# Moving loads, casts and DMA transposes in a one-core attention and feed-forward kernel, with the last sum cut into three

## The chip, the core and the metric

The kernel runs on one core of a Trainium2 chip. The core has a matrix engine (TensorE, PE in the profile), three engines for elementwise work (VectorE or DVE, ScalarE or ACT, GpSimd or POOL), a queue engine that only issues transfers (SyncE or SP) and 16 DMA engines. SP, ACT and POOL can each issue transfers, in the order of their own instruction streams. Products are summed in PSUM; everything else lies in SBUF.

The metric is the device time of one execution in microseconds (us). Before the change the median of three runs is 236.67 us (236.6 to 236.97). The profiled execution took 236.38 us.

## The reference

```python
scores = np.matmul(q, k.transpose(0, 1, 3, 2)) / np.sqrt(64)
# head h keeps all earlier positions where is_retrieval[h] is 1, else only the
# first 4 positions and the last 64
scores = np.where(mask, scores, -1e9)
a = softmax(scores)                       # over the keys
x = np.matmul(a, v)                       # 4 batches, 8 heads, 768 positions, 64 wide
x = x.transpose(0, 2, 1, 3).reshape(3072, 512)
h = x @ w_in                              # 512 -> 2048
g = h / (1 + np.exp(-beta * h))
out = g @ w_out                           # 2048 -> 512
```

All inputs and the output are float32. Heads 0, 2 and 6 are retrieval heads, the other five stream. The kernel works in bfloat16 with float32 sums.

## The kernel before

**Units and chunks.** A chunk is half a sequence of one batch (384 rows, three tiles of 128); there are 8. A unit is one chunk of one pair of heads, so chunk c holds units 4c to 4c+3, and there are 32. A unit goes through these steps, each with its instructions written out in the order in which they are to run:

- its keys and queries are cast to bfloat16 (`cast`, line 273), transposed on TensorE (`steps_T`, line 354), and copied from PSUM: keys by DVE (line 355), the two heads' queries by ACT and DVE (line 360). This holds for units 0 to 11;
- `sinks_of` (lines 337, 338) copies, on POOL, the key tiles of streaming heads with the four first positions put in;
- `steps_QK`: score products (line 419), for units 0 to 7 a second product that adds the mask (line 425), the exponential on ACT (line 428), and from unit 8 masks multiplied on DVE (lines 435, 440). A unit's products are cut into fills of up to four blocks;
- `values`: v is cast (`cast_v`, line 279) and, on POOL, the streaming heads' copy is made (lines 289, 290);
- `steps_PV`: products with v (line 463), 6 steps, one for each head and tile; after the last DVE takes reciprocals and divides, which writes x (line 468);
- x is transposed, on TensorE (`steps_X`, line 495) for units 0 to 7, 11, 30 and 31, and by a DMA transpose on SP (`x_by_dma`, line 479) for the others.

When the four units of a chunk have x transposed, its feed-forward part can run: `steps_G1` (16 groups of four products, line 518, in the order of the pairs of heads; tanh on ACT, line 521; the gate on DVE, line 524) and `steps_G2` (line 561 or 544, then ACT copies to one of three output buffers `osb`, and a transfer goes out).

**The ramp** is units 0 to 7, written out by hand (lines 690 to 807). Keys and queries of a chunk come in two groups of four heads (`load_qk`), v in three transfers on SP (`load_v`). With `held=True` a small POOL memset into the target keeps a transfer from starting before POOL gets there. w_in and w_out are cast in transfers that POOL issues (`load_w_in`, `load_w_out`, four quarters each). Ten products on zeros (line 167) run before the first data.

**The slots** follow: `for t in range(8, NU + 2)` (line 810). Slot t holds the score products of unit t, the products with v of unit t-1, and some feed-forward steps, in a merged order. From chunk 3 on the rows of keys and queries are loaded by POOL with a cast (`load_rows`, 3 transfers of keys and 6 of queries a chunk) and transposed by SP (`transposes_dma`, lines 323 and 326, three each).

**What sets the order.** Each engine runs its instructions in the order in which the program emits them. A call in the text of a slot's top is emitted there. `later(delay, fn)` puts work off until the program's own clock, which adds up a planned cost for each TensorE step, has moved by `delay`. `x_by_dma` is put off by 700 from the last step of the products with v, so it is emitted early in the next slot. A planner (`next_m`) picks feed-forward steps. It takes a chunk's first group only some time after its last x was emitted.

Of the kernel before, what the change touches and what calls it, by code (L numbers as in the profile page):

```python
# [17 lines left out]
def kernel(  # L18
# [86 lines left out]
    def load_qk(c, g, pairs=1, held=False):  # L105

        b, h2 = chunks[c]
        rows = slice(h2 * HALF, (h2 + 1) * HALF)
        both = stage.tile([128, 2, 2, 2, HT, D], F32, name=f"s{g}")
        for i, (name, src) in enumerate((("k", k), ("q", q))):  # L110
            staged[name, c, g] = both[:, i]
            if held:
                nc.gpsimd.memset(staged[name, c, g][:, 0, 0, 0, 0:1], 0.0)
        n = 2 // pairs
        for i in range(pairs):
            for name, src in (("k", k), ("q", q)):
                h = 4 * g + 2 * n * i
                eng = nc.scalar if pairs == 2 and name == "q" else nc.sync
                eng.dma_start(
                    out=staged[name, c, g][:, n * i:n * (i + 1)].rearrange("p a h t d -> p (a h) (t d)"),  # L120
                    in_=src[b, h:h + 2 * n, rows, :].rearrange("h (p t) d -> p h (t d)", t=HT))
# [26 lines left out]
    load_qk(0, 1)  # L148
# [19 lines left out]
    idle(10, ps_m, "mm")  # L168
# [26 lines left out]
    def negatives():  # L195
        nc.vector.tensor_scalar(out=Mc, in0=Nc, scalar1=0.0, scalar2=None, op0=ALU.is_ge)
        for i, m in enumerate([M0, Mo, Md, Mo, Md]):
            nc.vector.tensor_scalar(out=Ns[:, i * 128:(i + 1) * 128], in0=m, scalar1=-1.0, scalar2=-NEG, op0=ALU.add, op1=ALU.mult)
# [38 lines left out]
    def zero_q(i):  # L237
        for hh in range(2):
            nc.vector.memset(QTB[i][hh][half(1 - hh), :], 0.0)
# [6 lines left out]
    for i in range(3):  # L246
        zero_q(i)
    ones_v(nc.vector, 0)
    ones_v(nc.gpsimd, 1)
# [25 lines left out]
    def cast_v(u):  # L275
        b, h2, p = units[u]
        c = u // NPAIR
        copy = nc.scalar.copy if u in (1, 3) else nc.vector.tensor_copy if 8 <= u < 16 else nc.gpsimd.tensor_copy
        copy(out=VX[b % 2, p][:, h2 * HT:(h2 + 1) * HT, :, 0:D], in_=staged["v", c][:, :, 2 * p:2 * p + 2, :])  # L279
# [66 lines left out]
    def steps_T(u):  # L346
# [3 lines left out]
        def go():  # L350
# [7 lines left out]
            for hh in range(2):  # L358
                copy = nc.vector.tensor_copy if hh and u != 4 else nc.scalar.copy
                copy(out=QT[hh][half(hh), :].rearrange("p (j t) -> p j t", t=HT),  # L360
                     in_=tq[half(hh)].rearrange("p t j -> p j t"))
# [168 lines left out]
    def steps_G2(c):  # L530
# [3 lines left out]
        def part(ns, f0, cols=None):  # L534
            def go():
                for f in gates[c]:
                    f()
                if cols is not None:
# [7 lines left out]
                    if f0 + 4 == FO:  # L546
                        n0 = (2 * chunks[c][0] + chunks[c][1]) * HALF + ns * 128
                        m = (z - a) // 2 if z == d_model else z - a
                        osb = moe.tile([128, d_model], F32, name="osb", bufs=3)
                        nc.scalar.activation(out=osb[:, 0:m], in_=op[:, 0:m], func=ACTF.Copy, scale=0.5)  # L550
                        nc.scalar.dma_start(out=out[n0:n0 + 128, a:a + m], in_=osb[:, 0:m])
                        if m < z - a:
                            osb = moe.tile([128, d_model], F32, name="osb", bufs=3)
                            nc.vector.tensor_scalar(out=osb[:, 0:m], in0=op[:, m:z - a], scalar1=0.5, scalar2=None, op0=ALU.mult)
                            nc.sync.dma_start(out=out[n0:n0 + 128, a + m:z], in_=osb[:, 0:m])
# [13 lines left out]
        for ns in range(HT):  # L569
            if c == NCHUNK - 1 and ns == HT - 1:  # L570
                for cols in ((0, 256), (256, 512)):
                    res += [part(ns, f0, cols) for f0 in range(0, FO, 4)]
# [117 lines left out]
    cast_dp(0)  # L690
    load_v(0, held=True)
    load_qk(1, 0)
    negatives()
    transposes_of(0)
    st_u[0]["sinks"]()
    cast(1, "k", act)
    cast(1, "q")
# [7 lines left out]
    cast_dp(3)  # L705
    qk = steps_QK(1)
# [10 lines left out]
    load_qk(1, 1, held=True)  # L717
    st_u[3]["sinks"]()
    run(steps_QK(3))
    load_v(1, held=True)  # L720
    step((100, beta_go))
    values(0)
    load_w_in(0)
    cast_dp(4)
    values(1)
    values(2)
    cast(5, "q")
    values(3)


    run(steps_PV(0))
    transposes_of(4)
    cast(5, "k", act)
    run(steps_PV(1))
    step(steps_X(0)[0])
    qk = steps_QK(4)
    step(qk[0])
    run(steps_PV(2))
    step(qk[1])
    step(steps_X(1)[0])  # L740
    cast(6, "k", dve)
    transposes_of(5)
    step(qk[2])
# [66 lines left out]
    for t in range(8, NU + 2):  # L810
# [91 lines left out]
```

## Time and profile before

| What | Value |
|---|---|
| time, median of 3 runs | 236.67 us (236.6 to 236.97) |
| time of the profiled execution | 236.38 us |
| its span, first to last instruction | 234.7 us |
| TensorE busy | 224.9 us (96%) |
| ScalarE, VectorE, GpSimd busy | 158.9, 149.0, 102.9 us |
| granted TensorE clock, mean | 0.999 |
| DMA: read, written | 27.27 MB, 6.29 MB |
| first product on zeros, first transpose, first score product | 1.29, 5.53, 6.63 us |
| first products of unit 4 with v | 25.53 us |
| last product ends | 231.2 us |

The span is what the profiler sees between the first and the last instruction; the time has 1.7 us more around it. Times in the traces count from the start of the span. A line of the timeline gives start, duration, engine, line of the code, operation, output and inputs; several instructions of a kind in a row are merged, with their number behind an x. "Idle before" names what the engine waited for. The list of DMA issues gives the time from issue to landing.

### The profile page before, as it was taken

The numbers are of one execution on the slowest core, as the hardware profiler recorded it, in microseconds if no ns is written. First come the engines' busy times: TensorE is split into PE (matmuls) and PEld (weight loads), VectorE is DVE, ScalarE is ACT, GpSimd is POOL, SyncE is SP. The second block draws the span as 40 slices with busy tenths as digits, with TensorE's granted clock in tenths as the row PEclk, the third lists the DMA queues.
The fourth block names the chain that finished last, engine by engine and source line by source line (L and its number), as shares of the span: only waits on it lengthen the run. The fifth ranks groups of instructions, "written<-read, shape, count | busy, mean of one in ns | idle before, by whom it ended". The sixth has DMA issues, their size and how long they took to land.

```text
span 234.7 us, 5275 instructions
## 1 busy us (share of the span) xinstructions
PE 224.9 (96%) x1920; PEld 138.8 (59%) x1920; DVE 149.0 (64%) x384; ACT 158.9 (68%) x309; POOL 102.9 (44%) x246
## 2 busy tenths in 40 slices
PE   7797899999999999999999999999999999999994
PEld 3676766655666675656555666566665666555553
DVE  6778779877768598647862776476671857345400
ACT  2897888847767799558772779577875876266521
POOL 6487760357749932597078607841470000000000
PEclk9999999999999999999999999999999999999999
DMA  6999999999999999899989996999321200201112
GB/s 201 260 295 195 183 169 229 228 214 233 155 197 130 203 194 151 124 170 149 230 118 158 172 218 85 135 180 158 90 64 61 63 18 2 77 13 46 46 47 89
DMA packets 103530, 33.75 MB, mean 144 GB/s; under 512 B 89920, under 2 KB 100560, under 8 KB 103504
## 3 DMA queue, kind: packets, MB, share of 16 engines
q1 hardware_dynamic: 66976, 24.68, 51.2%
q0 software_dynamic: 35664, 8.13, 40.9%
q10 hardware_dynamic: 864, 0.60, 0.8%
q8 instruction: 15, 0.25, 0.5%
q14 instruction: 11, 0.09, 0.1%
HBM read 27.27 MB, written 6.29 MB: 143 GB/s over the span
## 4 chain that ended last, share of the span: by engine, by line
PE 81%; DMA 7%; DVE 6%; ACT 3%; POOL 1%; issue 1%; ACTq 0%; POOLq 0%
PE mm L518 28%; PE tp L561 25%; PE mm L561 9%; PE sp L419 9%; PE po L463 4%; DMA w_in_sb<-in_moe_w_in_dram 4%; DMA QTD<-s 3%; DVE gT L524 2%; PE mm L167 2%; PE sp L518 2%; PE tp L354 1%; ACT th L521 1%; DVE x L468 1%; ACT esL L428 1%; PE tp L544 1%
## 5 line engine op out<-in xcount | busy, mean ns | idle before, releaser
L518 PE MATMUL mm<-xT,w_in_sb 128*128 128x384 bf16 x488 | 93.4, 326 | 1.0 <-DVE gT L524 0.5
L521 ACT ACTIVATE th<-mm,beta_h 128x384 f32<-128x384 f32 x122 | 71.1, 583 | 24.1 <-PE mm L518 19.4
L524 DVE SCALAR_TENSOR_TENSOR gT<-th,mm 128x384 bf16<-128x384 f32 x122 | 66.7, 552 | 27.2 <-ACT th L521 23.8
L561 PE MATMUL tp<-w_out_sb,gT 128*128 128x512 bf16 x272 | 67.2, 379 | 0.0
L518 PEld LDWEIGHTS <-w_in_sb 128*128 128x128 bf16 x512 | 46.5, 98 | 27.0 <-issue 0.7
L561 PEld LDWEIGHTS <-gT 128*128 128x128 bf16 x368 | 33.3, 98 | 28.1
L428 ACT ACTIVATE esL<-sp 128x384 bf16<-128x384 f32 x72 | 37.8, 542 | 15.4 <-PE sp L419 15.3
L419 PE MATMUL sp<-QTD,KT 128*128 128x128 bf16 (+2 forms) x261 | 45.6, 242 | 1.7 <-ACT es L428 0.8
L428 ACT ACTIVATE es<-sp 128x512 bf16<-128x512 f32 (+1 forms) x56 | 30.4, 560 | 6.7 <-PE sp L419 5.4
L419 PEld LDWEIGHTS <-KT 128*128 128x128 bf16 x272 | 24.8, 98 | 9.3 <-DVE KT L355 0.7
L561 PE MATMUL mm<-w_out_sb,gT 128*128 128x512 bf16 x96 | 24.1, 379 | 0.0
L279 POOL CAST VX<-vs 128x384 bf16<-128x384 f32 x22 | 11.3, 512 | 28.5 <-issue 14.5
L312 POOL DMA_DIRECT2D s<-in_q_dram x30 | 22.3, 749 | 1.4 <-issue 0.9
L337 POOL COPY KO<-KT 128x128 bf16<-128x128 bf16 (+1 forms) x32 | 12.9, 405 | 14.5 <-DVE KT L355 9.3
L463 PEld LDWEIGHTS <-esL 128*128 128x128 bf16 x252 | 14.5, 98 | 7.2
L463 PEld LDWEIGHTS <-es 128*128 128x128 bf16 x220 | 13.9, 98 | 7.4 <-issue 0.2
L565 ACT ACTIVATE osb<-tp 128x512 f32<-128x512 f32 x17 | 10.2, 597 | 11.8 <-PE tp L561 11.5
L435 DVE TENSOR_TENSOR es<-es,Mh 128x512 bf16<-128x512 bf16 (+2 forms) x30 | 11.6, 388 | 8.5 <-ACT es L428 8.4
L440 DVE TENSOR_TENSOR esL<-esL,Mc 128x128 bf16<-128x128 bf16 x36 | 9.1, 252 | 12.0 <-ACT esL L428 12.0
L468 DVE TENSOR_TENSOR x<-po,rec 128x384 bf16<-128x384 f32 x28 | 15.6, 557 | 1.0
L463 PE MATMUL po<-VX,esL 128*128 128x65 bf16 x216 | 16.0, 193 | 0.0
L419 PE MATMUL sp<-QTD,KO 128*128 128x128 bf16 x79 | 14.7, 219 | 0.0
(94 smaller groups left out, 232.7 us busy)
## 6 DMA issues: line engine op xcount, KB each, us to landing
vs<-in_v_dram SPq DMA_DIRECT2D x24, 256.0 KB, 5.2
out_dram<-osb SPq DMA_DIRECT2D x23, 256.0 KB, 2.9
w_in_sb<-in_moe_w_in_dram POOLq DMA_DIRECT2D x4, 512.0 KB, 8.1
w_out_sb<-in_moe_w_out_dram POOLq DMA_DIRECT2D x4, 512.0 KB, 11.5
s<-in_k_dram SPq DMA_DIRECT2D x5, 384.0 KB, 5.0
s<-in_q_dram SPq DMA_DIRECT2D x5, 384.0 KB, 5.8
s<-in_k_dram POOLq DMA_DIRECT2D x15, 128.0 KB, 5.8
s<-in_q_dram POOLq DMA_DIRECT2D x30, 64.0 KB, 4.6
```

What stands on the lines that cost most here:

```text
L279: copy(out=VX[b % 2, p][:, h2 * HT:(h2 + 1) * HT, :, 0:D], in_=staged["v", c][:, :, 2 * p:2 * p + 2, :])
L312: nc.gpsimd.dma_start(out=ROWS[c % 2, "q"][:, t, :, 3 * D * hh:3 * D * hh + D], in_=q[b, hh:H:2, r:r + 128, :].rearrange("h p d -> p h d"))
L337: nc.gpsimd.tensor_copy(out=ko[:, ka - 1:kz - 1, :], in_=kt[:, ka * 128:kz * 128].rearrange("p (a j) -> p a j", a=n))
L419: nc.tensor.matmul(sp[:, (i - lo) * 128:(j - lo) * 128], lst[i][1], s["QT"][lst[i][0]][:, q0 * 128:(q0 + j - i) * 128], start=True, stop=n ...
L428: nc.scalar.activation(out=es[:, lo * 128:hi * 128], in_=sp[:, 0:w], func=ACTF.Exp, scale=scale)
L435: nc.vector.tensor_mul(es[:, a * 128:z * 128], es[:, a * 128:z * 128], Mh[h2][:, m0 * 128:(m0 + z - a) * 128])
L463: nc.tensor.matmul(po[:, qi, hh, :], e, val, start=(j == 0), stop=(j == len(lst) - 1))
L468: nc.vector.tensor_mul(x, po[:, :, :, 0:D], rec.to_broadcast([128, HT, 2, D]))
L518: nc.tensor.matmul(hp[:, 0:HALF], w_in_sb[:, mo, fi * 128:(fi + 1) * 128], xT[c][:, mo, :], start=(mo == 0), stop=(mo == MO - 1))
L521: nc.scalar.activation(out=th, in_=hp[:, 0:HALF], func=ACTF.Tanh, scale=beta_h[:, fi:fi + 1])
L524: nc.vector.scalar_tensor_tensor(out=gTs[c][:, fi, :], in0=th, scalar=1.0, in1=hp[:, 0:HALF], op0=ALU.add, op1=ALU.mult)
L561: nc.tensor.matmul(op, gTs[c][:, fi, ns * 128:(ns + 1) * 128], w_out_sb[:, fi, :], start=(fi == 0), stop=(fi == FO - 1))
```

## The change

**Loads.** Units 2 and 3, and units 4 and 5, get their keys and queries in two pairs of transfers, one for each unit, all on SP. The first quarter of w_in is issued behind unit 2's sinks. v's and units 6's and 7's transfers of chunk 1 are released at other places of POOL's stream.

**Casts.** Unit 0's queries go from POOL to ACT, unit 1's keys from ACT to DVE, unit 1's v from ACT to DVE, unit 4's queries from POOL to DVE, unit 6's keys from DVE to POOL. ACT copies both halves of unit 0's transposed queries. The negative masks are made in two parts, unit 2's query buffer is zeroed by POOL, and the columns of ones are written later.

**The order of the ramp.** Unit 4's transposes stand inside unit 0's products with v, unit 5's inside unit 2's, so the last of these, and the division behind it, come later. Unit 6's come ahead of unit 3's x. There are 8 products on zeros instead of 10.

**Slots.** The rows of chunk 4 are loaded in slots 10 and 11 (before: 11 to 13), those of chunks 5 to 7 one slot sooner. Chunk 3's key and query transposes both stand at the top of slot 9 (before: 9 and 10), chunk 4's at 12 and 13 (before: 13 and 14). For chunks 5 to 7 the keys stand at the top of slots 17, 21 and 25, the queries at 18, 22 and 26; before, both stood at the latter.

**The last sum.** The last 128 rows of the output are summed in column ranges of 256, 128 and 128, each in a PSUM bank of its own; ACT, DVE and ACT copy them. Before, there were two ranges of 256, and ACT and DVE each copied half of the second.

```diff
@@ load_qk and the first loads
-                eng = nc.scalar if pairs == 2 and name == "q" else nc.sync
+                eng = nc.scalar if (c, g) == (0, 0) and name == "q" else nc.sync
...
-    load_qk(0, 1)
+    load_qk(0, 1, 2)
...
-    idle(10, ps_m, "mm")
+    idle(8, ps_m, "mm")
@@ cast_v and steps_T
-        copy = nc.scalar.copy if u in (1, 3) else nc.vector.tensor_copy if 8 <= u < 16 else nc.gpsimd.tensor_copy
+        copy = nc.scalar.copy if u == 3 else nc.vector.tensor_copy if u == 1 or 8 <= u < 16 else nc.gpsimd.tensor_copy
...
-                copy = nc.vector.tensor_copy if hh and u != 4 else nc.scalar.copy
+                copy = nc.vector.tensor_copy if hh and u not in (0, 4) else nc.scalar.copy
@@ steps_G2, last 128 rows
-                        m = (z - a) // 2 if z == d_model else z - a
-                        osb = moe.tile([128, d_model], F32, name="osb", bufs=3)
-                        nc.scalar.activation(out=osb[:, 0:m], in_=op[:, 0:m], func=ACTF.Copy, scale=0.5)
-                        nc.scalar.dma_start(out=out[n0:n0 + 128, a:a + m], in_=osb[:, 0:m])
-                        if m < z - a:
-                            osb = moe.tile([128, d_model], F32, name="osb", bufs=3)
-                            nc.vector.tensor_scalar(out=osb[:, 0:m], in0=op[:, m:z - a], scalar1=0.5, scalar2=None, op0=ALU.mult)
-                            nc.sync.dma_start(out=out[n0:n0 + 128, a + m:z], in_=osb[:, 0:m])
+                        osb = moe.tile([128, d_model], F32, name="osb", bufs=3)[:, 0:z - a]
+                        if a == 256:
+                            nc.vector.tensor_scalar(out=osb, in0=op, scalar1=0.5, scalar2=None, op0=ALU.mult)
+                        else:
+                            nc.scalar.activation(out=osb, in_=op, func=ACTF.Copy, scale=0.5)
+                        (nc.scalar if z == d_model else nc.sync).dma_start(out=out[n0:n0 + 128, a:z], in_=osb)
...
-                for cols in ((0, 256), (256, 512)):
+                for cols in ((0, 256), (256, 384), (384, 512)):
@@ the ramp
-    cast_dp(0)
+    negatives((0, 1, 3))
+    cast(0, "k", dve)
+    cast(0, "q", act)
     load_v(0, held=True)
-    load_qk(1, 0)
-    negatives()
+    load_qk(1, 0, 2)
+    zero_q(2, nc.gpsimd)
+    negatives((2, 4))
     transposes_of(0)
+    cast(1, "k", dve)
+    cast(1, "q")
     st_u[0]["sinks"]()
-    cast(1, "k", act)
-    cast(1, "q")
...
     cast_dp(2)
     cast_dp(3)
+    load_qk(1, 1, held=True)
+    ones_v(nc.vector, 0)
+    ones_v(nc.gpsimd, 1)
...
     st_u[2]["sinks"]()
-    load_qk(1, 1, held=True)
+    load_w_in(0)
+    load_v(1, held=True)
     st_u[3]["sinks"]()
     run(steps_QK(3))
-    load_v(1, held=True)
+    cast(5, "k", act)
+    values(0)
+    values(1)
+    cast(4, "k", dve)
+    cast(4, "q", dve)
     step((100, beta_go))
-    values(0)
-    load_w_in(0)
-    cast_dp(4)
-    values(1)
     values(2)
-    cast(5, "q")
-    values(3)
-
-
-    run(steps_PV(0))
+
+
+    pv = steps_PV(0)
+    run(pv[:5])
     transposes_of(4)
-    cast(5, "k", act)
+    run(pv[5:])
     run(steps_PV(1))
-    step(steps_X(0)[0])
     qk = steps_QK(4)
     step(qk[0])
-    run(steps_PV(2))
+    cast(5, "q")
+    cast(6, "k")
+    values(3)
+    cast(6, "q")
+    pv = steps_PV(2)
+    run(pv[:5])
+    step(steps_X(0)[0])
     step(qk[1])
+    transposes_of(5)
+    run(pv[5:])
+    step(qk[2])
     step(steps_X(1)[0])
-    cast(6, "k", dve)
-    transposes_of(5)
-    step(qk[2])
     run(steps_PV(3))
     step(steps_X(2)[0])
     qk = steps_QK(5)
     step(qk[0])
     step(qk[1])
+    cast(7, "q")
+    load_w_in(1)
+    transposes_of(6)
     step(steps_X(3)[0])
     step(qk[2])
-    load_w_in(1)
-    cast(6, "q")
-    cast(7, "q")
     load_w_in(2)
     load_w_in(3)
-    transposes_of(6)
     cast(7, "k", dve)
@@ the slots
-            c, i = (t + 5) // NPAIR, (t + 5) % NPAIR
-            some = load_rows(c)[3 * i:3 * i + 3] if c < NCHUNK else []
-            if t < 14:
-                some = load_rows(4)[{9: 0, 10: 0, 11: 0, 12: 4, 13: 8}[t]:{9: 0, 10: 0, 11: 4, 12: 8, 13: 9}[t]]
+            c, i = (t + 6) // NPAIR, (t + 6) % NPAIR
+            some = load_rows(c)[3 * i:3 * i + 3] if t >= 14 and c < NCHUNK else []
+            if t in (10, 11):
+                some = load_rows(4)[0:4] if t == 10 else load_rows(4)[4:9]
         for i, f in enumerate(some):
-            later(1000 + (1500 if t > 14 else 1000) * i, f)
+            later((2500 if t == 10 else 1000) + (1500 if t > 14 else 1000) * i, f)
...
         if t == 9:
-            transposes_dma(3, "k")
-        if t == 10:
-            transposes_dma(3, "q")
+            transposes_dma(3)
+        if t == 12:
+            transposes_dma(4, "k")
         if t == 13:
-            transposes_dma(4, "k")
-        if t == 14:
             transposes_dma(4, "q")
+        if t > 14 and t % NPAIR == 1 and t // NPAIR + 1 < NCHUNK:
+            transposes_dma(t // NPAIR + 1, "k")
         if t > 14 and t % NPAIR == 2 and t // NPAIR + 1 < NCHUNK:
-            transposes_dma(t // NPAIR + 1)
+            transposes_dma(t // NPAIR + 1, "q")
```

The cut parts give `negatives` a list of the masks to make and `zero_q` the engine, and take the earlier calls of `zero_q` and `ones_v` out.

More of the change, by code (lines that the diff above doesn't have):

```diff
@@ L193, with negatives @@
     nc.gpsimd.affine_select(out=Nc, in_=Nc, compare_op=ALU.is_ge, fill=NEG, base=0, pattern=[[1, 128]], channel_multiplier=-1)
-    def negatives():
-        nc.vector.tensor_scalar(out=Mc, in0=Nc, scalar1=0.0, scalar2=None, op0=ALU.is_ge)
-        for i, m in enumerate([M0, Mo, Md, Mo, Md]):
+    def negatives(which):
+        if 2 in which:
+            nc.vector.tensor_scalar(out=Mc, in0=Nc, scalar1=0.0, scalar2=None, op0=ALU.is_ge)
+        for i in which:
+            m = [M0, Mo, Md, Mo, Md][i]
             nc.vector.tensor_scalar(out=Ns[:, i * 128:(i + 1) * 128], in0=m, scalar1=-1.0, scalar2=-NEG, op0=ALU.add, op1=ALU.mult)
@@ L235, in half, with zero_q @@
         return slice(hh * D, (hh + 1) * D)
-    def zero_q(i):
+    def zero_q(i, eng):
         for hh in range(2):
-            nc.vector.memset(QTB[i][hh][half(1 - hh), :], 0.0)
+            eng.memset(QTB[i][hh][half(1 - hh), :], 0.0)
     def ones_v(eng, b):
@@ L244, in ones_v @@
             eng.memset(VO[b, p][:, :, :, D:D + 1], 1.0)
[L246 to L249, printed above, removed]
+    zero_q(0, nc.vector)
+    zero_q(1, nc.vector)
     def masks_late(h2):
```

## The prediction

> **What bounds the kernel now.** I read the page's busy shares first, then a table of stretches, then TensorE's waits, then the SP queue's own order.
>
> ```profile
> span 234.7 us, 5275 instructions
> PE 224.9 (96%) x1920; PEld 138.8 (59%) x1920; DVE 149.0 (64%) x384; ACT 158.9 (68%) x309; POOL 102.9 (44%) x246
> ```
>
> TensorE (PE) is the bound. The stretches show where its other 4% lies (columns: length, then busy time of PE, its weight loads, DVE, ACT, POOL, granted clock, DMA share, GB/s):
>
> ```profile
> 2.00:34.00 32.00, 27.84 (x341) 20.06 (x340) 24.26 (x69) 24.71 (x52) 23.85 (x78) 1.00 1.14 232
> 34.00:90.00 56.00, 56.00 (x482) 34.83 (x481) 43.55 (x109) 42.69 (x84) 31.48 (x59) 1.00 1.36 196
> 90.00:120.00 30.00, 29.18 (x240) 17.72 (x239) 20.54 (x60) 21.00 (x42) 14.38 (x33) 1.00 1.38 159
> 120.00:228.00 108.00, 108.00 (x835) 63.28 (x834) 59.47 (x145) 69.32 (x132) 32.32 (x71) 1.00 0.59 93
> ```
>
> So 4.2 us are idle in the ramp (2 to 34), 0.8 between 90 and 120, nothing elsewhere until the tail. A faster engine elsewhere buys nothing; a new wait costs its full length. The 0.8 is these two waits:
>
> ```profile
> PE mm L518 <- DVE gT L524: 0.5, 1, 0.5
> PE sp L419 <- DMA QTD<-s: 0.3, 1, 0.3
> ```
>
> The second is unit 20's first product at 116.05: the product before it was issued at 115.54 and takes 0.03 of the stream, so the stream stands for 0.5 us.
>
> The change moves DMA transposes on SP, so I looked at what else SP carries. The transposes of x (line 479) feed the first matrix product of the feed-forward part (line 518). Two of them, each with SP's issue before or behind it:
>
> ```profile
> 72.87 1.18 SPq L479 DMA_TRANSPOSE xT<-x  x1
> 76.23 4.51 SPq L323 DMA_TRANSPOSE KT<-s  x3
> ...
> 121.18 0.36 SPq L567 DMA_DIRECT2D out_dram<-osb  x1
> 123.20 1.18 SPq L479 DMA_TRANSPOSE xT<-x  x1
> ```
>
> And PE's products that read them:
>
> ```profile
> 80.23 0.81 PE L518 MATMUL mm<-xT,w_in_sb 128*128 128x384 bf16 x4
> ...
> 128.25 0.81 PE L518 MATMUL mm<-xT,w_in_sb 128*128 128x384 bf16 x4
> ```
>
> The first is unit 10's: issued at 72.87, when x has just been written, it lands 5.6 later (the list of DMA issues, cut to that moment), at 78.5. Line 518 multiplies the four pairs in order, 0.16 us each, and needs pair 2 at 80.55: 2.1 us to spare. The second is unit 19's (landing 4.2, at 127.4); it is needed as fourth, at 128.74: 1.3 to spare.
>
> Last, the two DMA queues when both have work (18 to 20 us, kind, packets, MB, share of the 16 engines; q0 is POOL's, q1 is SP's):
>
> ```profile
> q0 software_dynamic: 381, 0.39, 116.8%
> q1 hardware_dynamic: 90, 0.02, 6.7%
> ```
>
> While w_in's first quarter flows, SP's transfers nearly stand, though v's last rows are still queued (they land after 23). The share over 2 to 34 is 1.14: the DMA engines are full in the ramp, and whatever is put first pushes something back.
>
> **The change, part by part.** One profiled execution, 236.38 us (span 234.7 and 1.7 around it), is the base; it lies 0.3 below the median of the three runs, 236.67.
>
> *Ramp, to unit 4.* With 8 idle products instead of 10, PE is free 2 x 0.425 = 0.85 earlier, at 4.7. Unit 0's queries are cast on ACT (idle from 3.4 to 6.1) when they land at 4.5: 0.5, as POOL took. Keys go at 4.7, queries at 5.05, ACT copies both halves of the transposed queries (2 x 0.4), and the first product starts at 6.0 instead of 6.63. Unit 1's keys, cast on DVE after the key copy (5.75 to 6.3) and its queries on POOL ahead of the sinks (landed 5.6), let its transposes go at 6.35, not at 7.05 and 7.60. Unit 2's land alone, so its casts follow at 7.85 (DVE) and 7.75 (POOL): transposes at 8.4, not 9.69. From there ACT sets the pace, as now: its last exponential ends at 13.4, not 14.65. Then v must land (12.4 at the latest row), and DVE casts v of unit 1 and unit 4's keys and queries, 3 x 0.5: unit 4's transposes go at 13.95, against 14.85. Up to here 0.9 to 1.25 us are won. The masks' parts, the zeroing on POOL (about 0.35 each, from 1.43 for 1536 columns) and the ones lie beside these casts; without that cover the ones on DVE cost unit 2's key copy 0.35.
>
> *Ramp, w_in.* Its first quarter is now issued behind unit 2's sinks on POOL, at about 10.25 instead of 13.76. It flows 2.2 to 3.7 us after its issue (rows at 19.68 and 13.76), so from 12.4 to 13.9, and takes about 2.7 us of the engines. On SP, units 4 and 5 are just through by 13; units 6 and 7, now 15.35 (keys) and 16.6 (queries), land up to 2.7 later, the queries at 19.2. POOL's queue stands behind them: unit 6's casts are ahead of unit 3's values and, behind these, of unit 5's sinks, unit 7's queries and the other three quarters of w_in. From 19.2: cast 0.5, unit 6 transposed at 19.75 (now 21.26); sinks and cast 1.0, three issues 2.25, unit 6's sinks done at 23.45 (now 23.3). So POOL's chain ends as it does now, while PE reaches unit 6's second block at 23.45 instead of 23.87, and unit 4's products with v at 24.6 instead of 25.53. I take 0.9 us for the whole ramp. Best: unit 6's queries land at 16.6, as now; PE's own work up to unit 6 then lets the chain start about 1.3 sooner: -2.2. Worst: they, or v, land 1.4 later: +0.5. Behind 34 us the transfers start at the old times, but the earliest that PE meets (unit 9's cast at 53.75 for 55.01) leaves 1.2, so the 0.9 is kept.
>
> *Dividing unit 2 later* moves DVE's 0.7 behind unit 5's key copy; its x is read after 18 us either way: 0.
>
> *Rows on POOL.* Nine issues of 0.75 to 0.88 move from the slots of units 11 to 13 to those of 10 and 11, later chunks one slot on. POOL idles 1.9 us at 65 and 6.4 at 89.5: 0 to +0.2, taken 0. Chunk 3's query transposes now follow its keys, from 62.7 to 66.8, ahead of an output at 63.74; there are three output buffers and the next two are filled at 69 and 74: 0.
>
> *Key transposes a slot sooner.* They are issued at the top of a slot, and the transpose of the last finished unit's x comes 700 units of the program's clock into it: on SP the x now stands behind three key transposes. Four places:
> - Chunk 4's before unit 10's x. SP is free at 72.5, three take 4.0 to 4.5 (58.72 and 76.23), x is issued at about 76.75. It lands 4.0 (median) to 6.0 later (unit 12's, behind three others at 88.71): 80.75 to 82.75, needed at 80.55. I take 4.8 and so +1.0; bounds 0 (a landing of 3.8, as at 68.4) and +2.4.
> - Chunk 6's before unit 19's x. SP is free at 121.54; 3.99; x at 125.55, and 4.1 as unit 20's took behind six: 129.65 against 128.74, +0.9; bounds 0 (2.4, as at 161.7) and +1.2.
> - Chunk 5's and 7's before units 15 and 23: SP is idle from 95.1 and from 145.54, so x is only 0.9 late, and 1.5 and 2.0 are to spare: 0, at most +0.3.
>
> *Query transposes* start 4 us sooner for chunk 5: unit 20's wait goes, -0.5; next there is the gate product, on time.
>
> *Tail.* Three banks: 32 products of 128 columns take 32 x 0.0556 = 1.78 where 16 of 256 take 16 x 0.109 = 1.74: +0.05. The last piece now waits on ACT for the output buffer that DVE waits for now, until 231.56; then 0.28, an issue, and 1.6 to landing as before: 0 (-0.3 if the lone last transfer lands faster, +0.2 if the buffer is later).
>
> Sum: -0.9 + 1.0 + 0.9 - 0.5 + 0.05 = +0.55: 236.9 for the base, 237.2 for the median.
>
> [...] The idle products start 0.425 apart, later ones of 512 columns 0.217 (the granted clock reads 1.00 in both): half rate, for 4.2 us from the first product at 1.29 to about 5.5. [...]
>
> **Rivals.** 0.2% (0.47 us) is about what a measurement of this kernel tells from none.
> - *The x land in time* (faster). SP's key transposes are done sooner, or x behind them lands in 3.8 and 3.2: both terms go, 0.55 - 1.9 = -1.35: 235.3. It decides at landings of 80.55 and 128.74. For it: landings of 2.3 to 4.0 us where DMA is quiet. Against: 4 to 6 behind other transposes.
> - *w_in does not hold SP back* (faster). Unit 6's queries land before 17.5, the ramp gives -2.2: 235.9. Against: the two queue lines above.
> - *The ramp gives nothing*: 238.1. Unit 6's queries come 1 us later still, and POOL's chain with them, or v does. For it: full DMA engines.
> - *Half rate to 9* (slower): if the stream of 8 does not do, and 4.2 us count anew from its end at 4.7, PE runs at half until 8.9. Its 2.4 us of work from 5.5 on then take twice as long; the waits that lie there now (0.56 + 0.21 + 0.69) cover more than half. Unit 4 falls back to 14.85, and since unit 6's queries set the rest, the ramp keeps 0.5: 237.6. Against: transposes and products follow the stream at once.
> - *The x come half as late*: the terms cancel, 236.7.
>
> **How the numbers follow.** My forecast 0.42 (0.06 of it within 0.2%; its own range 236.8 to 238.0), x in time 0.27, w_in harmless 0.12 (0.02 within), no ramp gain 0.08, half rate 0.04, cancelled 0.07. Faster 0.37, within 0.15, slower 0.48. The likeliest gives 237.2; 8 in 10 reach from 235.0 to 238.4.
>
> **What would show it.** Right: SP issues chunk 4's keys near 72.5 and unit 10's x near 76.8; PE waits on a DMA of xT near 80 and 128, about 1 us each; no wait on QTD near 115; unit 2's first transpose near 8.4; w_in's first quarter issued near 10, unit 6's queries landing near 19. Wrong: no wait on xT, or a first wait on w_in or on POOL's casts after 13 us that is longer than 1 us.

## The result and the profile after

The changed kernel takes 238.0 us (median; 236.5 to 240.0) against 236.2 us for the kernel before in the same comparison: a ratio of 1.0070 with a 95% interval of 1.0048 to 1.0092, slower by 0.7%. The forecast was 237.2, "slower" at 0.48. The profiled execution took 238.08 us (span 236.4), 1.70 more than that of before, where the forecast's sum was +0.55. In 5 of its 18 executions the granted clock has a mean of 0.986 or 0.993 instead of 0.999 or 1.000; their median is 239.8, that of the others 237.6. An experiment below shows what stood ahead of three falls of the clock (1.45, 0.55 and 0.52 us of PE's work in a stretch of 3.41); in these five executions the cause was not traced.

The page:

```profile
span 236.4 us, 5286 instructions
PE 223.3 (94%) x1911; PEld 138.4 (59%) x1934; DVE 149.0 (63%) x383; ACT 158.6 (67%) x309; POOL 103.7 (44%) x247
```

Of PE's 1934 products 23 have no record. Each leaves a hole of about 0.05 us (0.052 to 0.057 in the trace), so its busy time reads some 1 us low (an estimate: 23 times 0.05), and such a hole in a row of second products is no wait. The stretches, in the columns of the forecast's table:

```profile
2.00:34.00 32.00, 26.86 (x339) 19.61 (x338) 24.30 (x68) 25.29 (x52) 24.51 (x79) 1.00 1.11 227
34.00:90.00 56.00, 54.41 (x463) 33.67 (x467) 43.47 (x106) 41.37 (x81) 33.20 (x62) 1.00 1.56 200
90.00:120.00 30.00, 29.34 (x246) 18.03 (x248) 19.84 (x55) 20.84 (x43) 15.47 (x34) 1.00 1.30 168
120.00:228.00 108.00, 106.63 (x816) 62.77 (x828) 60.16 (x150) 69.74 (x134) 29.71 (x68) 1.00 0.54 88
```

From 34 to 90 PE, which stood nowhere before, now stands for 1.3 us (the two waits at 72.50 and 81.91 below; the rest of the 1.6 is such holes), while the DMA share rose from 1.36 to 1.56. PE's waits name what is new (total, times, longest):

```profile
PE tp L354 <- POOL qkb L273: 1.1, 1, 1.1
PE mm L518 <- DVE gT L524: 1.0, 2, 0.5
...
PE mm L518 <- DMA xT<-x: 0.7, 1, 0.7
...
PE sp L419 <- ACT esL L428: 0.6, 1, 0.6
```

Where they lie, from PE's timeline:

```profile
72.50 0.32 PE L419 MATMUL sp<-QTD,KT 128*128 128x384 bf16 x1 [0.61 <-ACT esL L428]
...
80.75 0.49 PE L518 MATMUL mm<-xT,w_in_sb 128*128 128x384 bf16 x2
81.91 0.49 PE L518 MATMUL mm<-xT,w_in_sb 128*128 128x384 bf16 x2 [0.67 <-DMA xT<-x]
...
129.12 0.81 PE L518 MATMUL mm<-xT,w_in_sb 128*128 128x384 bf16 x4
...
195.94 1.46 PE L518 MATMUL mm<-xT,w_in_sb 128*128 128x384 bf16 x8
197.90 0.81 PE L518 MATMUL mm<-xT,w_in_sb 128*128 128x384 bf16 x4 [0.50 <-DVE gT L524]
```

And SP's issues:

```profile
72.22 5.03 SPq L323 DMA_TRANSPOSE KT<-s  x3
77.34 1.21 SPq L479 DMA_TRANSPOSE xT<-x  x1
...
120.47 3.85 SPq L323 DMA_TRANSPOSE KT<-s  x3
124.41 1.21 SPq L479 DMA_TRANSPOSE xT<-x  x1
```

- *80.75*: unit 10's x, issued behind chunk 4's keys at 77.34, lands 4.5 later, at 81.86. It is read as third product, which waits.
- *72.50*: this is unit 12's first score product. Its own waits in the program are for an exponential and for three transposes. The exponential named is that of unit 11's last block (71.80 to 72.40), but before the change the same product started at 71.99 while that one still ran (71.93 to 72.53). The last of chunk 3's query transposes, issued at 66.11, landed 6.2 later, at 72.36. I read the wait as one for it; before, issued at 67.04, it took 4.8 and came at 71.86. Two loads of chunk 4's rows, which POOL now issues ahead of it, are under way beside it. SP's issues and POOL's, after and, behind the dots, before:

```profile
62.98 4.67 SPq L326 DMA_TRANSPOSE QTD<-s  x3
64.99 1.77 POOL L307 DMA_DIRECT2D s<-in_k_dram  x2
...
64.25 4.06 SPq L326 DMA_TRANSPOSE QTD<-s  x3
69.84 0.89 POOL L307 DMA_DIRECT2D s<-in_k_dram  x1
```

In the six traced kernels with the rows in their early slots this last transpose takes 5.8 to 6.9 us, in the eight with the old slots 4.8 to 5.0.
- *129.12*: unit 19's x, issued at 124.41, landed at 128.7 and is needed at 129.60. No wait, against the forecast.
- *197.90*: three groups of first products stand in a row; the third finds no free bank until DVE's gate is through, 0.50 us later.

Counted at the same products in both traces, the lateness of the changed kernel grows like this (us):

| Place | Forecast | Measured |
|---|---|---|
| ramp, at chunk 1's first product (33.34, now 33.22) | -0.9 | -0.12 |
| unit 12's queries, at chunk 2's first product (80.23, now 80.75) | 0 | +0.64 |
| unit 10's x, at chunk 3's first product (103.31, now 104.66) | +1.0 | +0.83 |
| from there to the last sum (227.55, now 229.67) | +0.4 | +0.77 |
| last sum to the end of the span (7.12, now 6.70) | +0.05 | -0.42 |
| sum | +0.55 | +1.70 |

The +0.4 is unit 20's -0.5 and unit 19's +0.9. The list of DMA issues says where the ramp's gain went. Its queue lines from 14 to 18 us (kind, packets, MB, share), after and before:

```profile
q0 software_dynamic: 499, 0.50, 73.8%
q1 hardware_dynamic: 642, 0.45, 42.7%
```

```profile
q1 hardware_dynamic: 2634, 0.99, 106.5%
q0 software_dynamic: 71, 0.07, 11.8%
```

w_in's first quarter (q0) now runs where the transfers of units 6 and 7 (q1) ran; unit 6's queries land at 20.00 instead of 16.59, POOL, whose next instruction casts them, stands until then, and w_in's other three quarters are issued at 21.44, 22.17 and 22.91 instead of 19.68, 21.31 and 22.05.

### The profile page after: what moved, and what is told of

Same layout as the page of the kernel before. It is cut to its first block, busy times and chain, and to the rows that moved or that the text cites. A ratio compares the mean times of both kernels' runs of the same rounds, so it can differ in the third digit from the quotient of the medians.

```text
span 236.4 us, 5286 instructions
## 1 busy us (share of the span) xinstructions
PE 223.3 (94%) x1911; PEld 138.4 (59%) x1934; DVE 149.0 (63%) x383; ACT 158.6 (67%) x309; POOL 103.7 (44%) x247
## 4 chain that ended last, share of the span: by engine, by line
PE 77%; DVE 7%; DMA 6%; ACT 4%; POOL 2%; issue 2%; POOLq 0%; ACTq 0%
PE mm L518 28%; PE tp L559 24%; PE sp L419 8%; PE mm L559 7%; PE po L463 4%; DMA s<-in_q_dram 4%; DVE gT L524 3%; DMA xT<-x 2%; PE sp L518 2%; PE tp L544 2%; PE mm L167 1%; ACT esL L428 1%; POOL w_in_sb L140 1%; DVE x L468 1%; ACT th L521 1%
## 5 line engine op out<-in xcount | busy, mean ns | idle before, releaser
L518 PE MATMUL mm<-xT,w_in_sb 128*128 128x384 bf16 x488 | 94.8, 326 | 2.3 <-DVE gT L524 1.0
L559 PE MATMUL tp<-w_out_sb,gT 128*128 128x512 bf16 x255 | 64.3, 379 | 0.8
L559 PE MATMUL mm<-w_out_sb,gT 128*128 128x512 bf16 x90 | 23.2, 379 | 0.2
L440 DVE TENSOR_TENSOR esL<-esL,Mc 128x128 bf16<-128x128 bf16 x36 | 10.5, 292 | 12.0 <-ACT esL L428 11.9
L435 DVE TENSOR_TENSOR es<-es,Mh 128x512 bf16<-128x512 bf16 (+2 forms) x30 | 11.6, 385 | 7.6 <-ACT es L428 7.5
L289 POOL COPY VO<-VX 128x64 bf16<-128x64 bf16 (+3 forms) x32 | 10.6, 331 | 9.7 <-DVE VX L279 8.3
```

Source lines behind the costliest of these rows:

```text
L289: nc.gpsimd.tensor_copy(out=vo[:, ka - 1:kz - 1, :, 0:D], in_=vx[:, ka:kz, h0:2, 0:D])
L435: nc.vector.tensor_mul(es[:, a * 128:z * 128], es[:, a * 128:z * 128], Mh[h2][:, m0 * 128:(m0 + z - a) * 128])
L518: nc.tensor.matmul(hp[:, 0:HALF], w_in_sb[:, mo, fi * 128:(fi + 1) * 128], xT[c][:, mo, :], start=(mo == 0), stop=(mo == MO - 1))
L559: nc.tensor.matmul(op, gTs[c][:, fi, ns * 128:(ns + 1) * 128], w_out_sb[:, fi, :], start=(fi == 0), stop=(fi == FO - 1))
```

## The experiments

All ratios are to the kernel before.

**The planner's count.** `next_m` weighs first against second products with `len(second) // NCHUNK`. Before, 100 // 8 is 12. The third bank makes the list 104 long, and the count 13, for every chunk. The kernel before with only that:

```diff
-n2 = sum(d <= done[0] for d in due) * (len(second) // NCHUNK) - done[1]
+n2 = sum(d <= done[0] for d in due) * 13 - done[1]
```

> The kernel before with only the planner's count raised to 13, which is what the third bank does to it unseen: the order of first and second products is then that of the changed kernel, all else as before. Theory 1 (the order costs): the wait on the gate at 197 us of the changed kernel appears here too, with the small ones beside it, and the time rises by 0.7 to 1.2, to 1.003 to 1.005. Theory 2 (the order is neutral by itself, and even gives unit 19's x more time): within 0.3 us.

Measured: 1.0049 (1.0028 to 1.0070). The first theory holds. From chunk 3's first product to the last sum PE takes 124.99 us (103.59 to 228.58); before it took 124.24, in the changed kernel 125.01. The 0.75 is a net figure: from chunk 6's first product on, PE takes 1.20 longer (47.45 against 46.25), and unit 20's wait, 0.5 before, is gone. The same wait on the gate appears:

```profile
194.85 1.46 PE L518 MATMUL mm<-xT,w_in_sb 128*128 128x384 bf16 x8
196.81 0.81 PE L518 MATMUL mm<-xT,w_in_sb 128*128 128x384 bf16 x4 [0.50 <-DVE gT L524]
```

The three banks alone, on the kernel before, copied by ACT, DVE and ACT as in the change, with the count written as 12:

```diff
-for cols in ((0, 256), (256, 512)):
+for cols in ((0, 256), (256, 384), (384, 512)):
...
-* (len(second) // NCHUNK) - done[1]
+* 12 - done[1]
```

> The kernel before with only the last sum in three banks, the planner's count held at 12, so that the order of products is the old one. Theory 1 (the tail itself gains): in the changed kernel the span ends 6.73 us after the first product of the last sum, in the kernel before 7.12; the time falls by 0.4, to 0.998 of the kernel before. Theory 2 (the tail as forecast, no gain): within 0.1 us, 1.000.

Measured: 0.9995 (0.9971 to 1.0020), which tells 0.4 us from nothing only barely; the profile has 6.93 from the last sum's first product to the end, 0.19 less than before. The changed kernel with the count of 12:

```diff
-* (len(second) // NCHUNK) - done[1]
+* 12 - done[1]
```

> The changed kernel, with the planner counting 12 second products for each chunk, as it did before. In the changed kernel the third bank makes the list of these products 104 long, and 104 // 8 is 13 where 100 // 8 was 12, so that the planner takes second products sooner and is left with up to nine first products in a row at each chunk's end. The restored count gives PE the old order of products. Theory 1 (the order costs): of the 2.1 us by which PE's last product is late, 1.35 stand at 105 us and 0.48 are won back at unit 20, so the order has cost 1.2; the wait on the gate at 197.9 goes, and the time falls by 0.7 to 1.2, to 1.002 to 1.004 of the kernel before. Theory 2 (the order is neutral, the loss comes from late x and keys): the time moves by less than 0.2 us.

Measured: 1.0062 (1.0031 to 1.0094), no gain over 1.0070 that could be told. Yet the second theory is not right either. With the old order the gate's wait at 197 is gone, and in its place stands the forecast's third term, which the changed kernel does not show. PE's waits and SP's issues:

```profile
PE mm L518 <- DMA xT<-x: 1.9, 1, 1.9
...
PE sp L419 <- DMA QTD<-s: 1.1, 1, 1.1
```

```profile
121.63 0.36 SPq L565 DMA_DIRECT2D out_dram<-osb  x1
122.08 3.87 SPq L323 DMA_TRANSPOSE KT<-s  x3
126.04 1.74 SPq L479 DMA_TRANSPOSE xT<-x  x1
```

Unit 19's x is issued at 126.04 (forecast 125.55), lands 5.2 later, and PE's fourth product waits 1.9. In the changed kernel the other order had put SP's output behind x (at 126.85) and the keys at 120.47, so that x landed 0.9 before its use. Two parts of the change hid each other.

**w_in's first quarter.** First at its old place on POOL, all else as changed:

```diff
 st_u[2]["sinks"]()
-load_w_in(0)
 load_v(1, held=True)
...
 values(0)
+load_w_in(0)
 values(1)
```

> The changed kernel with w_in's first quarter issued where it was before, behind unit 0's values on POOL. Theory 1 (w_in holds SP's transfers): unit 6's queries, 20.0 us in the changed kernel, land near 17; unit 6's second transpose goes at 19.2 instead of 20.62, the stream of the first product starts some 0.9 us earlier, and the time falls by 0.9, from 1.007 of the kernel before to 1.003. Theory 2 (they are late by the sum of all transfers, whichever goes first): the queries come no sooner than 19, or PE stands for w_in's first quarter in their place, and the time moves by less than 0.3 us.

Measured: 1.0022 (0.9998 to 1.0046). The queries land in time, from the lists of DMA issues at 11.0 to 11.25 us (KB each, us to landing) of the changed kernel and of this one:

```profile
s<-in_q_dram SPq DMA_DIRECT2D x1, 384.0 KB, 8.8
```

```profile
s<-in_q_dram SPq DMA_DIRECT2D x1, 384.0 KB, 5.5
```

But PE then waits 0.9 for w_in at 22.38, and the stream of first products is no earlier: chunk 1's first at 33.50. The gain, 1.1 us by the ratios and 1.23 between the two profiles, lies behind the ramp: neither unit 12's queries nor unit 10's x is waited for. (A part of the 1.1 may be the clock, which is 0.998 or more in all 12 executions.) w_in's other quarters go at 18.77 instead of 21.44, and from 58 to 70 us chunk 3's transposes land after 3.2 us (median, keys and queries) where the changed kernel has 5.0 and 5.1. The last of them, which unit 12 needs, still takes 6.2, but it is issued at 65.71 instead of 66.11 and lands at 71.87 instead of 72.36.

Ten idle products again:

```diff
-idle(8, ps_m, "mm")
+idle(10, ps_m, "mm")
```

> The changed kernel with ten idle products again. In 5 of its 18 runs the mean granted clock is 0.986 or 0.993, with a median of 239.8 us; in the other 13 it is 0.999 or 1.000, with a median of 237.6. Theory 1 (the shorter idle stream now and then leaves PE at half rate for longer): with ten, no run falls under 0.998, and the median is that of the undisturbed runs, 237.6, or less, because unit 6's queries at 20 us and not PE's start set the ramp's end; at most 0.85 is added if the ramp does follow PE's start. Theory 2 (the clock has nothing to do with it): about a quarter of the runs still show 0.986 to 0.993.

Measured: 1.0018 (0.9991 to 1.0045). One of 12 executions has a clock of 0.979, so the first theory's clause on the clock falls; a later kernel with ten idle products has 5 of 12 at 0.985 to 0.993. In its profiled execution w_in's quarter was issued at 11.36, behind unit 6's queries on SP (11.04), which landed at 16.32. That the two products did this is not shown: in a later kernel with ten it went at 10.44. In all profiled kernels with the changed ramp the landing goes with the order of these two issues. w_in's issue less that of the queries, and the queries' landing: -0.84, 20.00; -0.66, 19.55; -0.52, 19.52; -0.48, 19.82; then +0.05, 16.51; +0.13, 18.63; +0.32, 16.32; +0.67, 17.58; +0.77, 16.56; +0.88, 17.05; +1.92, 16.57. The two engines reach these issues within a microsecond of each other, and three kernels with ten idle products, the same up to there, fell on either side (+0.32, +0.05, -0.66).

**The slots.** Rows and DMA transposes of all chunks in their old slots, ramp and tail as changed:

```diff
-c, i = (t + 6) // NPAIR, (t + 6) % NPAIR
+c, i = (t + 5) // NPAIR, (t + 5) % NPAIR
...
-if t == 12:
+if t == 13:
     transposes_dma(4, "k")
...
+if t > 14 and t % NPAIR == 2 and t // NPAIR + 1 < NCHUNK:
+    transposes_dma(t // NPAIR + 1)
```

> The changed kernel with the rows' loads and the DMA transposes of all chunks in their old slots; ramp, tail and the planner's count stay as changed. Theory 1 (the slots cost): unit 12's wait for chunk 3's queries (0.78 of the stream at 72.5) and the wait for unit 10's x (0.83 at 81.9) go, unit 20's wait of 0.48 comes back: -1.1, 1.002 of the kernel before. Theory 2 (both waits come from the load on the DMA engines as a whole and reappear on other transfers): less than 0.3 us.

Measured: 1.0040 (1.0011 to 1.0070). Both waits are gone, as the first theory has it, and unit 20's is back, but longer:

```profile
116.74 0.32 PE L419 MATMUL sp<-QTD,KT 128*128 128x384 bf16 x1 [1.15 <-DMA QTD<-s]
```

Then x ahead of the keys, with ten idle products and the count of 12:

```diff
 if t == 12:
-    transposes_dma(4, "k")
+    later(800, lambda: transposes_dma(4, "k"))
...
-    transposes_dma(t // NPAIR + 1, "k")
+    later(800, lambda c=t // NPAIR + 1: transposes_dma(c, "k"))
```

> The changed kernel with ten idle products, the planner's count of 12, and the key transposes of chunks 4 to 7 given to SP 800 units of the program's clock into their slot, so that they stand behind the transpose of x and not ahead of it. Theory 1 (SP's order makes x late): with the count of 12 alone, unit 19's x was waited for 1.9 us at 131; here neither unit 10's nor unit 19's x is waited for, no run falls under a clock of 0.998, the gate at 197 is on time, and the time is 235.5, 0.996 of the kernel before. Theory 2 (x is late because the DMA engines are full, whatever the order): a wait for x of over 0.5 us stays, and the time is at or above that of the kernel before.

Measured: 1.0016 (0.9989 to 1.0043). No x of unit 10 or 19 is waited for, but chunk 5's queries, issued from 104.33 on beside POOL's rows of chunk 6, take 8.3 to 9.4 us to land, the last at 117.59, and PE stands 2.5 us for them, until 117.72. (The profile names a transfer of x there, but that lands at 117.81, when the product has started.) This is one execution, of 239.44 us against a median of 236.92; the others need not show this wait. In stretches of 3.41 us (columns as above):

```profile
115.19:118.61 3.42, 1.02 (x7) 0.56 (x7) 1.68 (x5) 1.07 (x2) 0.00 (x0) 1.00 1.38 246
118.61:122.02 3.41, 3.41 (x15) 1.76 (x14) 1.23 (x5) 1.07 (x2) 2.08 (x5) 0.50 0.72 141
```

After the stall the clock is half for one such stretch, to 122.02. The same, with unit 2's x read later by PE:

```diff
 run(steps_PV(3))
-step(steps_X(2)[0])
 qk = steps_QK(5)
 step(qk[0])
 step(qk[1])
+step(steps_X(2)[0])
```

> As the kernel with x ahead of the keys, and PE takes unit 2's x behind the second block of unit 5 instead of ahead of its first. In the changed kernel PE stands 1.15 at 18.41 for unit 2's division, which is now behind unit 5's copies on DVE. Theory 1 (this stall is on the path once unit 6's queries land at 16 to 17 us): 0.6 to 1.0 less than the kernel without the swap. Theory 2 (it only shifts the stall to the next reader, unit 6's transposes or unit 1's x): within 0.2 of it.

Measured: 1.0009 (0.9979 to 1.0039), within the interval of the one without it. Its profiled execution drew the late landing (19.55), so unit 6's transposes took the stall over; this run does not decide.

**What brought the clock down.** A kernel without late transfers (the old slots with the mended ramp, next) with four stalls set in:

```diff
+def stall(n):
+    nothing = ps_m.tile([128, 512], F32, name="mm")
+    nc.tensor.matmul(nothing[:, 0:128], zeros[:, 0:128], zeros[:, 0:128], start=True, stop=True)
+    nc.vector.tensor_copy(out=scr, in_=nothing[:, 0:128])
+    for _ in range(n):
+        nc.gpsimd.tensor_copy(out=scr, in_=zeros[:, 0:128])
+    nc.tensor.matmul(nothing[:, 0:128], scr, zeros[:, 0:128], start=True, stop=True)
...
+if t in (25, 27, 29, 31):
+    stall({25: 2, 27: 4, 29: 6, 31: 8}[t])
```

> The kernel with old slots and four stalls of PE set into the slots of units 25, 27, 29 and 31: an idle product, a copy of it on DVE, a chain of 2, 4, 6 and 8 copies on POOL, and a product that reads the last. Each should stop PE for about 0.7 us and 0.35 for each copy: 1.4, 2.1, 2.8 and 3.5, some 8 to 10 us in all. Theory 1 (a stall of PE brings its clock down): in the kernel with x first PE stood 2.5 us at 117.7, and from 118.6 the granted clock was half for 3.4 us; in the changed kernel with the count of 12 it stood 1.9 and stayed at full rate. Then the longer stalls, 2.8 and 3.5, are followed by 3.4 us of half rate, the 1.4 is not, and the mean clock is 0.986 to 0.993. Theory 2 (the drops come from elsewhere, such as the time of the first products): the clock stays at 0.998 or more.

Measured: 253.1 us, clock 0.98 in every execution. The half-rate times begin at 149.65, 183.78 and 204.26, that is 34.13 and 20.48 apart, 10 and 6 times 3.413, and the clock reads 0.50 for the 3.41 us behind each; the second table is cut on that grid. First the ends of the stalls, from PE's timeline (in brackets the wait before each):

```profile
149.04 0.23 PE L177 MATMUL mm<-zeros,scr 128*128 128x128 bf16 x1 [1.97 <-POOL scr L176]
167.36 0.23 PE L177 MATMUL mm<-zeros,scr 128*128 128x128 bf16 x1 [2.45 <-POOL scr L176]
184.19 0.29 PE L177 MATMUL mm<-zeros,scr 128*128 128x128 bf16 x1 [3.27 <-POOL scr L176]
203.74 0.23 PE L177 MATMUL mm<-zeros,scr 128*128 128x128 bf16 x1 [3.88 <-POOL scr L176]
```

The stretches:

```profile
146.23:149.65 3.42, 1.45 (x13) 0.78 (x12) 2.01 (x7) 0.83 (x3) 2.61 (x6) 1.00 1.23 158
149.65:153.06 3.41, 3.41 (x14) 1.49 (x13) 0.00 (x0) 0.91 (x2) 2.93 (x7) 0.50 0.65 47
163.30:166.71 3.41, 1.61 (x18) 0.86 (x16) 2.13 (x6) 0.79 (x2) 0.64 (x3) 1.00 0.94 180
166.71:170.13 3.42, 2.77 (x23) 1.85 (x24) 0.67 (x2) 2.14 (x5) 1.38 (x5) 1.00 0.71 182
180.37:183.78 3.41, 0.55 (x5) 0.23 (x3) 1.59 (x5) 0.27 (x1) 1.47 (x5) 1.00 0.14 29
183.78:187.19 3.41, 3.00 (x10) 1.29 (x11) 0.00 (x0) 0.71 (x2) 3.10 (x9) 0.50 0.00 0
200.85:204.26 3.41, 0.52 (x4) 0.36 (x5) 0.00 (x0) 0.09 (x1) 2.36 (x8) 1.00 0.14 29
204.26:207.67 3.41, 3.41 (x15) 1.70 (x13) 0.71 (x2) 2.05 (x4) 0.00 (x0) 0.50 0.00 0
```

The first theory holds, with a correction: in this run the fall goes not with the stall's length but with the work left in a stretch of the grid. Stretches with 1.45, 0.55 and 0.52 us of work were followed by half rate. The second stall, 2.45 against the first's 1.97, straddles two stretches (1.61 and 2.77 busy), and the clock stays. The other traces that were cut on a grid of 3.413 fit. In that of before the clock's records begin at 5.61, at full rate, and fall to half at 234.31, behind PE's last product; in that of the changed kernel this is 4.49 and 236.60. The distances, 228.70 and 232.11, are 67 and 68 times 3.413. The stretches ahead of these two falls hold 0.31 and 0.17 us of work; in all others of the two traces PE is busy for 2.06 or more, and the clock reads 1.00. In the kernel with x first 1.02 was followed by half rate; in the changed kernel with the count of 12 1.50 was not. The price is of the right size: this span is 18.0 us longer than that of the kernel with old slots, the four waits are 11.6 of it, and three stretches at half rate would be 5.1 (an estimate: half of 3 times 3.41).

**A faster kernel.** The changed ramp and tail with the old slots, the count of 12, and w_in's quarter a little later:

```diff
 st_u[2]["sinks"]()
-load_w_in(0)
 load_v(1, held=True)
 st_u[3]["sinks"]()
+load_w_in(0)
```

> The changed ramp and tail alone, mended: rows and DMA transposes in their old slots, the planner's count 12, eight idle products, and w_in's first quarter issued behind unit 3's sinks on POOL, about 1.2 us later than in the changed kernel, so that unit 6's queries are put on their queue first. Theory 1 (the ramp's loss is w_in's place alone): unit 6's queries land at 16.3 to 16.6 as in the runs where w_in came after them, w_in's other quarters go at 18.8 instead of 21.4, PE's stream of first products starts 0.5 to 1.0 sooner than before, and the tail gives 0.1 to 0.4: 235.2 to 235.8, 0.994 to 0.997 of the kernel before. Theory 2 (the ramp is bound by all its transfers together, and unit 20's late queries take the gain back at 116): within 0.4 us of the kernel before.

Measured: 235.35 us, 0.9950 (0.9933 to 0.9968): faster than both kernels. The queries land at 17.58, w_in's quarter at 21.17, chunk 1's first product comes at 32.56 instead of 33.34, and the last sum takes 6.73 to the end: 0.78 and 0.39 together are the 1.2 us by which the profiled execution (235.17) is under that of before. Unit 20 waits 0.2. With chunks 5 to 7's transposes a slot sooner and the rows where they were:

```diff
+if t > 14 and t % NPAIR == 1 and t // NPAIR + 1 < NCHUNK:
+    later(800, lambda c=t // NPAIR + 1: transposes_dma(c, "k"))
 if t > 14 and t % NPAIR == 2 and t // NPAIR + 1 < NCHUNK:
-    transposes_dma(t // NPAIR + 1)
+    transposes_dma(t // NPAIR + 1, "q")
```

> As the kernel with old slots, but chunks 5 to 7 have their key transposes a slot sooner, behind x, and their query transposes first in the next slot; the rows stay in their old slots. Theory 1 (chunk 5's queries were late at 117 in the kernel with x first because POOL's rows, a slot early, shared the DMA engines with them): with the rows where they were, the last of these queries lands before 115 instead of 117.6, unit 20 waits for nothing, unit 19's x is on time, and the time is 0.5 below that of the kernel with old slots. Theory 2 (the transposes are slow by themselves, 6 us and more for three of queries in a row): the wait at 116 stays over 0.5 us and the two kernels are equal within 0.2.

Measured: 0.9943 (0.9922 to 0.9965), the same. The last of chunk 5's queries is issued at 109.31 and lands at 115.49; with the old slots it is issued at 108.91 and lands at 115.11. An earlier start of the keys brings these no sooner. The three take 6.2 to 7.2 us here, against 8.3 to 9.4 in the one profile with the rows a slot early, and unit 20 waits 0.2, as with the old slots. And unit 2's x later, with the edit shown above, on the old slots:

> As the kernel with old slots, with unit 2's x taken by PE behind the second block of unit 5 instead of ahead of its first. In that kernel PE stands 1.19 at 18.82 for unit 2's division and 0.64 at 20.58. Theory 1 (unit 2's late division is on the path now that unit 6's queries land at 17.6): PE's stream of first products starts 0.4 to 1.0 sooner, and the time is 0.4 to 1.0 below the kernel with old slots. Theory 2 (unit 6's queries, cast at 18.1, or the next x take the stall over): within 0.2 of it.

Measured: 0.9948 (0.9925 to 0.9971), the same: the second theory, though its profiled execution, its slowest (queries at 18.63), can't show which reader took the stall over in the others.

## Why the prediction was right, and where not

The side was right, and the forecast's own range, 236.8 to 238.0, held the median at its very edge. The size was not right: +1.70 between the profiles, three times the +0.55, and the sum was right for only a part of its reasons.

*Unit 10's x, +1.0*: right, with its mechanism. SP issued the keys at 72.22 (forecast 72.5), x at 77.34 (76.75), it landed 4.5 later (4.8), and cost 0.83. It goes when keys and rows are put back, and also when the transposes land sooner.

*Ramp, -0.9*: measured -0.12, inside its bounds. Unit 6's queries landed at 20.00, not 19.2, and PE's transposes of them went at 20.62, not 19.75. This is the rival "the ramp gives nothing", which had 0.08. That its 238.1 lies near the measured 238.0 is luck: it holds unit 19's 0.9, which is not there, and neither unit 12's 0.64 nor what the new order of products costs. The forecast's own sign of being wrong is met as well: PE waits 1.09 us for POOL's cast of unit 6 at 20.62. The mechanism, w_in's flow in front of SP's, was in the text, its size 0.8 short. What failed is a sentence behind it: "Behind 34 us the transfers start at the old times". They did not. w_in's quarters were up to 1.8 late on POOL, w_out's last landed at 47.80 instead of 47.01, and with w_in at its old place (its quarters sooner, w_out's last at 46.67) the last of chunk 3's queries lands 0.5 sooner. Where w_in is issued behind the queries with room, and PE needn't wait for it, the ramp gives 0.78.

*Unit 12's wait, +0.64*: missing. The prediction priced chunk 3's queries and the earlier rows at 0, from output buffers and POOL's own time. It didn't ask what the rows do to the transfers under way, nor whether the last of the queries still lands by 71.99: before the change it had 0.13 to spare. With the rows beside it, it takes 6.2 instead of 4.8, which is more than the 0.9 by which it starts sooner. The wait needs both faults. With early rows it is 0.6 to 1.1 in the three profiles in which unit 6's queries land late, and 0.2 or nothing in the three in which they land in time; with old slots it is 0.14 at most.

*Unit 19's x, +0.9*: not there, but not wrong as a mechanism. It was 1.9 with the old order of products, and hidden by the new one, though not in every run: 0.4 of it shows in the profile with ten idle products.

*Unit 20's queries, -0.5*: right in number, wrong in cause. Issued 1.9 sooner, the last landed at 115.81 (before 115.91); PE only came later. The kernel before with the count of 13 loses this wait too, with its transposes where they were.

*Tail, +0.05*: measured -0.42 in this execution, under the bound of -0.3, with the interval of the run that has it alone reaching from -0.7 to +0.5. The step that failed is another: the prediction priced the three banks' products and not the length of the list that holds them. The new order costs 0.75 net in the profile of the run with the count alone, 0.7 to 1.7 in its time.

*The x half as late*: this rival's sum is wrong. Half of 1.9 taken off +0.55 is -0.4, so 236.3, and not 236.7. It stays within the 0.47 that counts as none.

*Half rate to 9*: didn't happen in the profiled execution. The products of the stream of 8 start 0.43 apart up to 4.26, and from 5.80 the products go at full rate (0.17 for 384 columns). The clock's records begin, at full rate, at 5.61 with ten idle products (before) and at 4.49 with eight. That 4.2 us could count anew from the end of the stream was the author's estimate; no run shows it. What the forecast lacks is the lower mean clock of five executions; the other 13 have a median of 237.6. In the run with the stalls the stretches followed by half rate weren't idle: one held 1.45 us of work. By these numbers a wait of 2 us that lies in one stretch of the grid, and leaves 1.41 of it for work, costs up to 1.7 us on top (an estimate: half of 3.41).

## What to carry to other kernels

A transfer's place in a queue is priced by what lands later for it, down the whole backlog: ask of each transfer with little to spare, before the change, when it lands and who reads it. Here w_in's first quarter moved ahead of unit 6's queries, which landed at 20.00 instead of 16.59, and w_out's last quarter at 47.80 instead of 47.01. When a list gets longer, look for what else is computed from its length, a planner's shares above all. When a load is moved, price what it does to the transfers then under way, and not only the time of the engine that issues it (here a transpose took 6.2 us to land instead of 4.8). And two faults of one change can hide each other, so a part that shows no cost in the sum may show it once another is mended.

## What was not expected of the hardware

- In the eleven traces with the changed ramp, unit 6's queries, put on SP's queue 0.5 to 0.8 us behind POOL's first quarter of w_in, landed at 19.5 to 20.0; put 0.05 to 1.9 us ahead of it, at 16.3 to 18.6.
- The last DMA transpose of chunk 3's queries, which took 4.8 to 5.0 us to land with the rows in their old slots, took 5.8 to 6.9 when two loads of rows, issued by POOL within 1.3 us of it, were under way (before 4.8, after 6.2).
- In the run with the stalls, stretches of the 3.413 us grid with 1.45, 0.55 and 0.52 us of PE's work were followed by one at half rate, and so was one with 1.02 in the kernel with x first; with 1.61 (the stalls) it was not, nor with 1.50 in the changed kernel with the count of 12 (its wait of 1.9; grid counted back from the fall at 237.52). One stretch at half rate takes 0.007 off the mean clock (an estimate: half of 3.41 in 236; the profiled execution with x first, which has one, reads 0.993), so the 0.993 and 0.986 of the changed kernel's slower executions fit one and two of them. That those too followed waits for transfers was not traced; that one did, at 117.7, was.
